# The 1e-9 added to the sums of a softmax on GpSimd instead of VectorE, in a kernel with a fixed order of instructions

## The chip, the cores and the metric

One NeuronCore of a Trainium2 chip runs the kernel. The metric is the device time of one execution in microseconds (us), as the median of several runs. The engines are TensorE (PE; its weight loads are listed apart as PEld), VectorE (DVE), ScalarE (ACT), GpSimd (POOL) and SyncE (SP), which issues all the DMAs here.

## The reference

Causal attention with a decay for 8 batches of 8 heads, 576 positions, 64 numbers a head, and behind it a mixer over tokens and over channels, all in float32:

```python
scores = scale * np.matmul(q, k.transpose(0, 1, 3, 2))
log_f = np.log(np.clip(f, 0.0001, 1.0))
cum = np.cumsum(log_f, axis=-1)
decay = cum[:, :, :, None] - cum[:, :, None, :]
scores = np.where(causal, -1000000000.0, scores + decay)
scores = scores - np.max(scores, axis=-1, keepdims=True)
attn = np.exp(scores)
attn = attn / (np.sum(attn, axis=-1, keepdims=True) + 1e-09)
out = np.matmul(attn, v)
# x: the heads side by side, 576 x 512 a batch
h = np.maximum(x.transpose(0, 2, 1) @ w_tok1, 0.0) @ w_tok2
u = x + h.transpose(0, 2, 1)
y = u + np.maximum(u @ w_ch1, 0.0) @ w_ch2
```

The 1e-9 in the last line of the softmax is what the change is about.

## The kernel before, in words

Nearly every product is made with both factors split into a high part, in TensorE's fast 32-bit format, and a low part, the rest: three matmuls where one would be (high by high, low by high, high by low). The first four heads are done in plain float32.

For each of the 64 heads, `build` describes the following steps. SP loads q and k (`raw`); their high and low parts are made (L972, L980 on GpSimd, L970 on ScalarE) and gathered by DMA into the tiles `k1`, `k2`. TensorE makes the scores of five blocks of rows, of 64 or 128 rows and 64, 192, 320, 448 and 576 columns (L1061). VectorE adds the mask and takes each row's minimum of the negated scores (`rmin`, L1068). ScalarE makes the exponentials into `pr` and their sums into `sums` (`expo`, L1075). `rec1` (L1093) adds 1e-9 to the head's five columns of sums, in a tile of 128 x 6; `rec2` (L1096) takes the reciprocals; `norm` (L1103), on GpSimd, multiplies the five blocks of exponentials by them in place. TensorE transposes the blocks (L1117); ScalarE copies out the high halves and VectorE the low ones (L729, L738); GpSimd puts the low half of the first block below its high half (L732); TensorE multiplies by the values (L1189 to L1201); ScalarE and VectorE fold the result into `xt` (L1239, L1246). Behind every four heads the token mixer of half a batch is mixed in between, and behind every eight a part of the channel mixer (L1683 to L1815). From some 562 us on only products with the channel mixer's weights are left (L1339 and on, then L1544 to L1546 and L1606 to L1608).

`rec` and `sums` exist four times (`sm = n % 4`), `pr` three times.

The order on each engine is worked out by the program while it is built. Every step is given to `Plan.op` with its engine, an assumed duration, a priority, what it reads and writes, and its buffers. `Plan.run` plays the engines' time with these assumed durations; whenever an engine is free it takes, of the steps that are ready and find their buffers, the one with the lowest priority. The instructions are then written in that order, so each engine's queue is fixed and worked off in order. The priorities come from the table `PR`: one row for each kind of step (k23, k24 and so on, numbered as the kinds appear), with one number for each of its occurrences.

Where the plan sees TensorE without work for long, the kernel writes filler matmuls, `idle` (L803), of 128 columns whose result nobody reads. Their number follows from the length of the planned gap:

```python
gap = (o.start - at_) * heads
g0, g1, g2 = GAP if o.start > 50000 else EARLY
for _ in range(PRM["FILL"] if at_ == 0 else int((gap - g0) / g1) if gap > g2 else 0):
    E["idle"](at_ == 0)
```

Of the kernel before, what the change touches and what calls it, by code (L numbers as in the profile page):

```python
# [13 lines left out]
ALU = mybir.AluOpType  # L14
# [9 lines left out]
    k0=(1,),  # L24
    k1=(1, 0,),
# [18 lines left out]
    k21=(5, 6,),
    k22=(9, 10, 21, 29,),
    k23=(1, 0, 2, 5, 4, 3, 7, 10, 6, 22, 14, 20, 29, 25, 24, 36, 37, 35, 49, 51, 53, 56, 58, 52, 73, 75, 79, 91, 89, 88, 103, 106, 105, 114, 117, 115, 135, 136, 133, 145, 149, 146, 165, 167, 171, 179, 183, 185, 199, 203, 200, 213, 215, 217, 226, 230, 228, 240, 241, 243, 260, 263, 262, 275, 280, 279, 291, 293, 297, 309, 315, 310, 322, 326, 323, 341, 346, 343, 359, 358, 363, 373, 374, 375, 387, 394, 390, 407, 409, 405, 422, 425, 424, 437, 439, 438, 451, 452, 459, 464, 467, 472, 485, 491, 486, 503, 502, 501, 518, 523, 521, 534, 535, 536, 551, 555, 553, 564, 566, 568, 587, 590, 589, 605, 607, 608, 620, 621, 619, 635, 639, 636, 652, 655, 657, 667, 677, 672, 686, 689, 688, 700, 709, 707, 725, 721, 720, 737, 735, 739, 752, 755, 756, 764, 766, 768, 780, 787, 783, 805, 806, 803, 812, 814, 820, 826, 839, 831, 846, 863, 861, 857, 859, 876, 879, 892, 889, 893, 898, 906, 911, 923, 922, 925, 929, 937, 942, 950, 951, 954, 964, 953,),
    k24=(18, 14, 17, 20, 22, 30, 26, 29, 23, 28, 38, 40, 41, 34, 37, 60, 48, 49, 55, 57, 69, 61, 64, 59, 62, 76, 77, 79, 75, 78, 92, 93, 96, 95, 97, 101, 102, 107, 94, 98, 118, 120, 121, 123, 124, 139, 134, 137, 133, 135, 153, 157, 159, 154, 156, 161, 167, 170, 165, 169, 186, 187, 189, 183, 184, 194, 201, 203, 200, 202, 219, 220, 222, 225, 226, 233, 237, 238, 239, 241, 255, 259, 260, 256, 258, 269, 270, 273, 272, 274, 284, 287, 290, 286, 288, 298, 299, 303, 300, 302, 321, 323, 325, 322, 324, 333, 340, 342, 338, 341, 353, 355, 357, 360, 361, 372, 378, 379, 374, 376, 384, 391, 392, 385, 389, 403, 408, 409, 405, 407, 424, 421, 423, 427, 428, 437, 441, 443, 440, 442, 457, 459, 461, 455, 458, 470, 472, 475, 468, 471, 491, 493, 495, 492, 494, 505, 507, 510, 506, 509, 520, 522, 523, 526, 528, 543, 535, 539, 542, 545, 556, 560, 562, 557, 559, 576, 578, 580, 571, 574, 591, 596, 597, 594, 595, 608, 609, 611, 610, 616, 628, 632, 633, 629, 631, 639, 643, 645, 646, 647, 664, 667, 670, 665, 668, 679, 680, 681, 682, 683, 692, 694, 697, 693, 696, 707, 715, 717, 712, 716, 731, 736, 738, 734, 737, 748, 756, 757, 752, 753, 767, 769, 771, 768, 770, 780, 786, 787, 784, 785, 801, 797, 799, 796, 798, 812, 809, 811, 813, 815, 827, 829, 831, 830, 832, 837, 840, 842, 843, 846, 856, 861, 862, 859, 860, 878, 879, 881, 876, 877, 884, 890, 891, 895, 896, 901, 909, 911, 906, 908, 916, 932, 934, 931, 933, 929, 928, 930, 942, 944, 947, 962, 964, 956, 959, 961, 965, 966, 975, 977, 979, 989, 992, 988, 990, 993, 995, 997, 1006, 1007, 1010, 1018, 1019, 1021, 1023, 1026, 1034, 1036, 1022, 1025,),
# [5 lines left out]
    k30=(35, 32, 34, 46, 51, 50, 66, 65, 64, 84, 81, 83,),  # L53
# [64 lines left out]
    k95=(524,),  # L118
# [1977 lines left out]
```

## Time and profile before

| | |
|---|---|
| median of 3 runs | 1024.95 us (1023.31 to 1025.09) |
| the profiled execution | 1024.19 us, its span 1022.4 us |
| TensorE busy | 1009.8 us (99%) |
| VectorE busy | 810.8 us (79%) |
| ScalarE busy | 695.1 us (68%) |
| GpSimd busy | 421.7 us (41%), none of it after some 565 us |
| DMA queue of SP | 210.99 MB, 61.6% of the 16 engines' span |
| granted TensorE clock | 1.000 |

The span runs from the first to the last instruction of the trace. The shares are averages over the whole span. The kernel has two parts with different limits, so the busy time by stage is the view to start from. An engine's idle time matters only where something later waits for it; for that there are the lists of who waited for whom, and the timeline.

### The profile page before, as it was taken

How to read it: one execution, taken by the hardware profiler on the slowest of the kernel's cores; microseconds unless marked ns; L12 is line 12 of the kernel's file. 1: busy time of each engine (PE TensorE's matmuls, PEld its weight loads, DVE VectorE, ACT ScalarE, POOL GpSimd, SP SyncE). 2: the span in 40 equal slices, each digit the busy share in tenths (PEclk: the TensorE clock that was granted, in tenths of full speed). 3: DMA queues.
4: the chain of work that ended last, by engine and by line, in shares of the span. 5: the costliest groups of instructions: out<-in, count | busy, mean ns of one | idle time of the engine just before them, and what ended most of it. 6: DMA issues, size and time to landing. Idle time of an engine off the chain costs nothing.

```text
span 1022.4 us, 19342 instructions
## 1 busy us (share of the span) xinstructions
PE 1009.8 (99%) x6230; PEld 883.1 (86%) x6230; DVE 810.8 (79%) x1932; ACT 695.1 (68%) x1708; POOL 421.7 (41%) x530
## 2 busy tenths in 40 slices
PE   9999999999999999999999999999999999999998
PEld 7588999999899999999999988888888788888886
DVE  7789889898899797887896557859669765976794
ACT  6898889888888788888886434565365446544652
POOL 6589778778787686887872100000000000000000
PEclk9999999999999999999999999999999999999999
DMA  8766798786877766553655468916832772384054
GB/s 239 252 203 215 278 305 290 280 271 235 278 250 277 278 215 225 186 206 130 237 187 211 185 189 267 298 48 211 276 104 78 224 224 82 124 250 152 21 175 145
DMA packets 110597, 212.23 MB, mean 208 GB/s; under 512 B 13296, under 2 KB 51184, under 8 KB 109472
## 3 DMA queue, kind: packets, MB, share of 16 engines
q1 hardware_dynamic: 110496, 210.99, 61.6%
q8 instruction: 50, 0.82, 0.3%
q14 instruction: 51, 0.42, 0.1%
HBM read 113.26 MB, written 44.04 MB: 154 GB/s over the span
## 4 chain that ended last, share of the span: by engine, by line
PE 84%; ACT 5%; DVE 5%; DMA 2%; issue 2%; POOL 1%; SPq 1%; POOLq 0%; DVEq 0%; ACTq 0%
PE bank L1117 8%; PE bank L1606 6%; PE bank L1544 6%; PE bank L1545 6%; PE bank L1546 6%; PE bank L1607 6%; PE bank L1608 6%; PE bank L1061 5%; PE pair L1199 3%; PE pair L1061 3%; PE pair L1201 3%; ACT pr L1075 2%; PE bank L1785 2%; PE bank L1787 2%; PE bank L1786 2%
## 5 line engine op out<-in xcount | busy, mean ns | idle before, releaser
L1103 POOL TENSOR_SCALAR pr<-pr,rec 128x192 f32<-128x192 f32 (+4 forms) x320 | 166.7, 536 | 68.0 <-DVE rec L1096 25.9
L729 ACT ACTIVATE p<-bank 128x384 fp32r<-128x384 f32 (+3 forms) x300 | 129.8, 473 | 21.5 <-PE bank L1117 19.4
L1117 PE MATMUL bank<-ident,pr 128*128 128x128 f32 (+1 forms) x960 | 139.6, 275 | 1.3 <-DVE p L738 0.4
L1075 ACT ACTIVATE pr<-bank,nmin 128x448 f32<-128x448 f32 (+3 forms) x256 | 118.0, 469 | 17.3 <-DVE nmin L1068 15.8
L1117 PEld LDWEIGHTS bank<-ident,pr 128*128 128x128 f32 (+1 forms) x960 | 106.3, 131 | 18.4 <-ACT pr L1075 2.2
L1068 DVE CUSTOM_DVE_ANT_0 bank<-bank,mask 128x448 f32<-128x448 f32 (+3 forms) x256 | 106.0, 434 | 13.6 <-PE bank L1061 8.4
L738 DVE TENSOR_TENSOR p<-bank,p 128x384 fp32r<-128x384 f32 (+1 forms) x180 | 104.6, 589 | 13.1 <-ACT p L729 12.3
L1606 PE MATMUL bank<-ring,w2r 128*128 128x512 f32 x242 | 94.4, 390 | 0.7 <-ACT ring L729 0.7
L1607 PE MATMUL bank<-ring,w2r 128*128 128x512 f32 x242 | 94.2, 389 | 0.0
L1608 PE MATMUL bank<-ring,w2r 128*128 128x512 f32 x220 | 85.6, 389 | 0.0
L1061 PE MATMUL bank<-k 128*128 128x320 f32 (+1 forms) x480 | 83.4, 302 | 1.6 <-ACT part L1820 1.1
L1201 PE MATMUL pair<-p,vv 128*128 128x512 f32 x240 | 75.5, 322 | 0.0
L980 POOL TENSOR_TENSOR hl<-raw,hl 128x1152 fp32r<-128x1152 f32 x27 | 72.6, 2689 | 1.4
L1199 PE MATMUL pair<-p,vv 128*64 128x512 f32 x240 | 69.4, 330 | 0.0
L1061 PEld LDWEIGHTS bank<-k 128*128 128x128 f32 (+1 forms) x480 | 63.0, 176 | 5.8 <-ACT part L1820 1.5
L729 ACT ACTIVATE ring<-h 128x512 fp32r<-128x512 f32 x73 | 44.3, 628 | 34.6 <-PE bank L1607 17.2
L729 ACT ACTIVATE ring<-xt 128x512 fp32r<-128x512 f32 (+1 forms) x84 | 53.0, 648 | 19.9 <-DVE xt L1754 6.2
L738 DVE TENSOR_TENSOR low<-bank,p 64x512 fp32r<-64x512 f32 (+1 forms) x120 | 52.3, 444 | 12.0 <-ACT p L729 10.1
L1075 ACT ACTIVATE pr<-pair,nmin 128x576 f32<-128x576 f32 x64 | 47.3, 739 | 17.9 <-DVE nmin L1068 15.5
L729 ACT ACTIVATE ring<-bank 128x512 fp32r<-128x512 f32 (+2 forms) x96 | 47.4, 498 | 14.5 <-PE bank L1717 6.7
L735 POOL TENSOR_TENSOR ring<-xt,ring 128x576 fp32r<-128x576 f32 x32 | 46.1, 1449 | 23.5 <-ACT ring L729 23.4
L1606 PEld LDWEIGHTS bank<-ring,w2r 128*128 128x128 f32 x242 | 45.4, 188 | 10.7 <-ACT ring L729 1.1
(200 smaller groups left out, 3050.3 us busy)
## 6 DMA issues: line engine op xcount, KB each, us to landing
k<-hl SPq DMA_DIRECT2D x180, 288.0 KB
w2r<-sd SPq DMA_DIRECT2D x80, 256.0 KB
raw<-in_qk SPq DMA_DIRECT2D x60, 288.0 KB
w2r<-wd SPq DMA_DIRECT2D x60, 256.0 KB
vr<-in_v SPq DMA_DIRECT2D x32, 320.0 KB
ud<-xt SPq DMA_DIRECT2D x8, 1152.0 KB
pd<-part SPq DMA_DIRECT2D x32, 288.0 KB
dd<-in_w_ch SPq DMA_DIRECT2D x12, 512.0 KB
```

Of the source, the lines that this page charges most:

```text
L729: nc.scalar.activation(out, in_, func, scale=scale)
L738: nc.vector.tensor_tensor(out, in_, asf(hi), op=ALU.subtract)
L1061: nc.tensor.matmul(ps[:m, of : of + w], k[:, 0, i0 : i0 + m], k[:, 1, j0 : j0 + w], start=(x == 0), stop=(fq or x == 1))
L1068: nc.vector.tensor_tensor_reduce(x, x, E["mask"][:m, a : a + w], -1.0 / D**0.5, 3e38, op0=ALU.add, op1=ALU.min, accum_out=E["nmin"][sm][:m ...
L1075: nc.scalar.activation(at(pr)[:m, poff[t] : poff[t] + w], at(buf)[:m, of : of + w], AF.Exp, bias=E["nmin"][sm][:m, t : t + 1], scale=-1.0, ...
L1103: nc.gpsimd.tensor_scalar(x, x, r, 0.0, op0=ALU.mult, op1=ALU.add)
L1117: nc.tensor.transpose(out, at(pr)[:, poff[i] + start[j] : poff[i] + end[j]], E["ident"])
L1199: nc.tensor.matmul(x[:D], at(vv)[:, v0 + j, :D], at(pb)[:, 1, c0 : c0 + w], start=False, stop=last)
L1201: nc.tensor.matmul(x, at(vv)[:, v0 + j, :], at(pb)[:, 0, c0 : c0 + w], start=False, stop=last)
L1606: nc.tensor.matmul(o_, wh[:, ms], h_, start=first and pr == 0, stop=False, skip_group_check=not first)
L1607: nc.tensor.matmul(o_, wl[:, ms], h_, start=False, stop=False, skip_group_check=not first)
L1608: nc.tensor.matmul(o_, wh[:, ms], l_, start=False, stop=pr == PH - 1, skip_group_check=not first)
```

## The change

`rec1` is given to GpSimd, with a second operation (adding 0.0) that its form there has, and an assumed duration of 190 in place of 72. The table `PR` is another one in nearly every row.

```diff
 PR = dict(
...
-    k0=(1,),
-    k1=(1, 0,),
...
+    k0=(0,),
+    k1=(0, 1,),
...
         def rec1(sm=sm):
-            nc.vector.tensor_scalar(E["rec"][sm][:, :, :2], E["sums"][sm].rearrange("p (a b) -> p a b", b=3), 1e-9, None, op0=ALU.add)
+            nc.gpsimd.tensor_scalar(E["rec"][sm][:, :, :2], E["sums"][sm].rearrange("p (a b) -> p a b", b=3), 1e-9, 0.0, op0=ALU.add, op1=ALU.add)
...
-        p.op("DVE", 72, n + o["rec"], rec1, rd=[("sums", sm, t) for t in range(NS)], wr=[("rec", sm)])
+        p.op("POOL", 190, n + o["rec"], rec1, rd=[("sums", sm, t) for t in range(NS)], wr=[("rec", sm)])
         p.op("DVE", 100, n + o["rec"], rec2, wr=[("rec", sm)])
```

`rec1` has a row of its own there (k26), with one number for each head. What the table does to the order shows on the engines' queues. In the rows below, names carry the number of the tile: `rec_92` is the third of the four `rec` tiles, `pr_184` the third `pr` tile, `bank_63` to `bank_66` the four single PSUM banks, `pair_70` and `pair_71` the double ones.

VectorE at the fifteenth head, before:

```order
L738 TENSOR_TENSOR low_191<-bank_64,p_190 64x512
L738 TENSOR_TENSOR p_189<-bank_63,p_189 128x512
L1093 TENSOR_SCALAR rec_92<-sums_88 128x3x2
L1096 RECIPROCAL rec_92<-rec_92 128x3x2
L741 SCALAR_TENSOR_TENSOR ring_162<-bank_66,ring_161 128x288
L738 TENSOR_TENSOR p_187<-bank_64,p_187 128x384
L1068 ISA pair_70,nmin_85<-pair_70,mask 128x576
L1068 ISA nmin_85 128x1
```

and now:

```order
L738 TENSOR_TENSOR p_189<-bank_66,p_189 128x512
L833 TENSOR_SCALAR dd<-dd 128x512
L1068 ISA pair_70,nmin_85<-pair_70,mask 128x576
L1068 ISA nmin_85 128x1
L738 TENSOR_TENSOR low_191<-bank_63,p_190 64x64
L1246 SCALAR_TENSOR_TENSOR xt_151<-pair_71,lower,xt_151 128x576
L1096 RECIPROCAL rec_92<-rec_92 128x3x2
L738 TENSOR_TENSOR p_185<-bank_65,p_185 128x384
```

The add (L1093) is gone from VectorE's queue, and the reciprocal (L1096) stands behind the minimum of the next head's largest block and the fold into `xt`; the instruction behind it is now the subtraction for the low half (L738). In 37 of the 64 heads L738 is the next instruction after the reciprocal.

GpSimd at the same head, before:

```order
L972 TENSOR_SCALAR hl_175<-raw_172 128x2x576
L980 TENSOR_TENSOR hl_175<-raw_172,hl_175 128x2x576
L1103 TENSOR_SCALAR pr_184<-pr_184,rec_92 128x448
L1103 TENSOR_SCALAR pr_184<-pr_184,rec_92 128x320
L732 TENSOR_SCALAR p_190<-low_191 64x576
L1103 TENSOR_SCALAR pr_184<-pr_184,rec_92 64x64
L1103 TENSOR_SCALAR pr_184<-pr_184,rec_92 128x576
L980 TENSOR_TENSOR vv_181<-vr_174,vv_181 128x10x64
L1103 TENSOR_SCALAR pr_184<-pr_184,rec_92 128x192
```

and now:

```order
L972 TENSOR_SCALAR hl_175<-raw_172 128x2x576
L980 TENSOR_TENSOR hl_175<-raw_172,hl_175 128x2x576
L1093 TENSOR_SCALAR rec_92<-sums_88 128x3x2
L732 TENSOR_SCALAR p_190<-low_191 64x576
L1103 TENSOR_SCALAR pr_184<-pr_184,rec_92 128x448
L1103 TENSOR_SCALAR pr_184<-pr_184,rec_92 128x320
L1103 TENSOR_SCALAR pr_184<-pr_184,rec_92 64x64
L1103 TENSOR_SCALAR pr_184<-pr_184,rec_92 128x576
L980 TENSOR_TENSOR vv_181<-vr_174,vv_181 128x10x64
L1103 TENSOR_SCALAR pr_184<-pr_184,rec_92 128x192
```

The add has come in between the subtraction of 1152 columns (L980) and the copy of the low half (L732), which is ahead of the head's first multiplication. Of the 64 adds, 11 stand right behind an L980 of 1152 columns, 6 behind one of the values' (640 columns) and 10 behind an L735; in 37 heads the first multiplication follows the add at once.

TensorE in front of the token mixer's transposes (L1683) of the second batch's second half, before:

```order
L1740 MATMUL bank_64<-held,ring_157 128x288
L1741 MATMUL bank_64<-held,ring_157 128x288
L1742 MATMUL bank_64<-held,ring_158 128x288
L1740 MATMUL bank_64<-held,ring_157 128x288
L1741 MATMUL bank_64<-held,ring_157 128x288
L1742 MATMUL bank_64<-held,ring_158 128x288
L1199 MATMUL pair_71<-p_187,vv_180 64x384
L1201 MATMUL pair_71<-p_187,vv_180 128x384
L1683 MATMUL bank_66<-ident,xt_151 128x128 x4
L1683 MATMUL bank_65<-ident,xt_151 128x128 x4
```

and now:

```order
L1061 MATMUL bank_66<-k_177 128x320
L1061 MATMUL bank_66<-k_179 128x320
L1061 MATMUL bank_66<-k_177 128x192
L1061 MATMUL bank_66<-k_179 128x192
L1117 MATMUL bank_63<-ident,pr_184 128x128 x3
L803 MATMUL pair_71<-lower 16x128 x21
L1683 MATMUL bank_64<-ident,xt_151 128x128 x4
L1189 MATMUL pair_71<-p_190,vv_180 128x512
L1190 MATMUL pair_71<-p_190,vv_180 128x64
```

The matmuls of the token mixer (L1740 to L1742) and of the attention that came ahead of these transposes stand elsewhere now, and 21 fillers have come in. In all there are 204 fillers instead of 168: the first 140 and the last 16 as before, and between them groups of 15, 5, 7 and 21 where there were 7 and 5.

## Rows read from the trace of the kernel before

**Rows 1.** The page's first part: busy us, share of the span, instructions.

```profile
PE 1009.8 (99%) x6230; PEld 883.1 (86%) x6230; DVE 810.8 (79%) x1932; ACT 695.1 (68%) x1708; POOL 421.7 (41%) x530
```

**Rows 2.** Busy time by stage (us, then PE, PEld, DVE, ACT, POOL; clock, DMA share).

```profile
0.00:28.00 28.00, 25.79 (x202) 19.07 (x203) 21.82 (x70) 19.96 (x56) 17.84 (x35) 1.00 0.87 242
...
60.00:562.00 502.00, 496.47 (x3796) 466.66 (x3795) 431.65 (x1249) 421.63 (x1165) 380.13 (x463) 1.00 0.68 238
...
1018.00:1022.40 4.40, 0.55 (x3) 0.13 (x1) 0.69 (x1) 0.00 (x0) 0.00 (x0) 1.00 0.32 119
```

**Rows 3.** What TensorE waited for, 28 to 562 us: total, times, longest.

```profile
PE bank L1061 <- ACT part L1820: 1.1, 1, 1.1
PE bank L1740 <- DVE p L738: 0.9, 2, 0.6
...
PE pair L803 <- ACT xt L1232: 0.3, 1, 0.3
...
PE pair L1189 <- POOL p L732: 0.2, 1, 0.2
PE pair L1189 <- DVE xt L1246: 0.2, 1, 0.2
```

**Rows 4.** The same of the weight loads, 28 to 562 us.

```profile
PEld bank L1117 <- POOL pr L1103: 0.8, 1, 0.8
```

**Rows 5.** TensorE in order of time at the fillers: start, us, [idle before].

```profile
60.59 0.58 PE L803 MATMUL pair<-lower 128*16 128x128 f32 x7 [0.25 <-ACT xt L1232]
...
364.13 0.54 PE L803 MATMUL pair<-lower 128*16 128x128 f32 x5
364.99 0.66 PE L1683 MATMUL bank<-ident,xt 128*128 128x128 f32 x4 [0.33 <-DVE p L738]
...
563.57 1.10 PE L803 MATMUL pair<-lower 128*16 128x128 f32 x16
564.51 0.37 PE L1740 MATMUL bank<-held,ring 128*128 128x288 f32 x1
```

**Rows 6.** Add and reciprocal on VectorE by form: busy us, mean ns | idle before.

```profile
L1096 DVE RECIPROCAL rec<-rec 128x6 f32<-128x6 f32 x64 | 11.9, 186 | 1.4
...
L1093 DVE TENSOR_SCALAR rec<-sums 128x6 f32<-128x6 f32 x64 | 9.8, 153 | 11.7 <-ACT pr L1075 11.1
```

**Rows 7.** GpSimd's instructions by form: busy us, mean ns | idle before.

```profile
L980 POOL TENSOR_TENSOR hl<-raw,hl 128x1152 fp32r<-128x1152 f32 x27 | 72.6, 2689 | 1.4
...
L732 POOL TENSOR_SCALAR p<-low 64x576 fp32r<-64x576 f32 x60 | 40.1, 668 | 30.6 <-DVE low L738 15.6 <-DVE rec L1096 5.8 <-ACT xt L1239 4.5
...
L972 POOL TENSOR_SCALAR hl<-raw 128x1152 fp32r<-128x1152 f32 x27 | 31.2, 1156 | 4.9 <-DMA k<-hl 3.6 <-issue 0.4 <-DMA vr<-in_v 0.3
...
L1103 POOL TENSOR_SCALAR pr<-pr,rec 64x64 f32<-64x64 f32 x64 | 21.4, 335 | 13.8 <-ACT p L729 5.6 <-PE bank L1117 4.6 <-DVE rec L1096 3.2
...
L2082 POOL MEMSET const-float32-0.0<- 128x1 f32 x1 | 0.1, 103 | 0.2 <-issue 0.2
```

**Rows 8.** Two heads' reciprocals in order of time: start, us, [idle before].

```profile
20.82 0.19 DVE L1096 RECIPROCAL rec<-rec 128x6 f32<-128x6 f32 x1
...
21.21 0.82 POOL L1103 TENSOR_SCALAR pr<-pr,rec 64x64 f32<-64x64 f32 x2 [0.15 <-DVE rec L1096]
...
118.54 2.98 POOL L980 TENSOR_TENSOR hl<-raw,hl 128x1152 fp32r<-128x1152 f32 x1
...
121.35 0.16 DVE L1093 TENSOR_SCALAR rec<-sums 128x6 f32<-128x6 f32 x1
...
121.54 0.19 DVE L1096 RECIPROCAL rec<-rec 128x6 f32<-128x6 f32 x1
```

**Rows 9.** What GpSimd and VectorE waited for, whole span: total, times, longest.

```profile
POOL pr L1103 <- DVE rec L1096: 25.9, 16, 5.4
...
DVE rec L1093 <- ACT pr L1075: 11.1, 18, 1.6
```

**Rows 10.** TensorE's only gap between 139.5 and 143 us, in order of time.

```profile
141.97 0.47 PE L1189 MATMUL pair<-p,vv 128*128 128x512 f32 x1 [0.15 <-DVE xt L1246]
```

More of the change, by code (lines that the diff above doesn't have):

```diff
@@ L149 @@
-    k126=(1365, 1369, 1371, 1373, 1374, 1363, 1366, 1368, 1370, 1372,),
+    k8=(7,),
+    k9=(0, 1,),
+    k10=(2, 5, 4, 6,),
+    k11=(1, 3, 7, 8, 9, 10,),
+    k12=(2, 4, 5, 6, 7, 13, 14, 18, 24, 29, 34, 37, 38, 39, 40, 43, 50, 51, 58, 57, 60, 63, 61, 62, 91, 111, 123, 124, 122, 121, 127, 126, 129, 125, 144, 149, 184, 183, 182, 172, 173, 181, 180, 186, 202, 211, 223, 225, 224, 220, 240, 244, 242, 239, 273, 288, 293, 290, 291, 292, 310, 313, 312, 311, 329, 339,),
+    k13=(3, 5, 10, 11, 14, 17, 23, 30, 37, 43, 53, 56, 62, 68, 84, 102, 101, 180, 183, 202, 213, 250, 252, 290, 302, 333, 349, 368, 397, 441, 472, 480, 511, 536, 563,),
@@ new lines @@
+    k14=(5, 8, 13, 16, 21, 25, 31, 42, 44, 50, 61, 64, 75, 78, 96, 118, 120, 193, 203, 218, 234, 276, 266, 326, 325, 358, 370, 390, 437, 482, 499, 530, 532, 565, 611,),
+    k15=(9, 10, 15, 19, 24, 27, 33, 45, 51, 52, 62, 66, 79, 98, 100, 135, 177, 204, 206, 230, 244, 278, 277, 345, 327, 359, 389, 481, 450, 483, 516, 546, 564, 581, 613,),
+    k17=(7, 8, 12, 15, 20, 21, 28, 40, 47, 46, 58, 60, 81, 103, 100,),
+    k18=(11, 12, 13, 14, 15, 16, 24, 34, 38, 37, 40, 45, 58, 71, 73,),
+    k19=(11, 23, 48, 59, 71, 77, 90, 103, 114, 143, 160, 179, 195, 213, 232, 258, 272, 286, 303, 328, 345, 355, 373, 392, 408, 422, 438, 455, 464, 478, 492, 503,),
@@ new lines @@
+    k43=(116, 168, 233, 296, 377, 426, 505, 543, 618, 656, 736, 776, 849, 898, 965, 978,),
+    k44=(117, 176, 246, 308, 392, 446, 527, 566, 643, 689, 767, 811, 880, 932, 996, 1009,),
+    k45=(95, 92, 91, 98, 147, 149, 151, 152, 222, 236, 215, 243, 276, 278, 277, 284, 360, 361, 366, 372, 415, 412, 416, 417, 500, 494, 504, 505, 547, 537, 539, 540, 627, 629, 622, 631, 666, 658, 659, 669, 765, 751, 747, 752, 796, 794, 798, 795, 904, 879, 890, 882, 934, 938, 933, 939, 1012, 1007, 1009, 1008, 1021, 1020, 1022, 1023,),
@@ new lines @@
+    k74=(573, 583,),
+    k75=(110, 150, 212, 289, 338,),
+    k76=(194, 226, 273, 317, 347, 396, 467, 500, 560, 597,),
+    k77=(211, 260, 307, 346, 388, 421, 500, 547, 612, 627,),
+    k78=(130, 161, 194, 210, 243, 259, 301, 330, 361, 371,),
+    k79=(128, 185, 241, 309, 362,),
+    k80=(381, 382, 383, 384, 529, 530, 531, 544, 545, 547,),
+    k81=(938, 939, 940, 970, 972, 966, 968, 987, 985, 995,),
+    k82=(975, 978, 977, 1000, 1004, 997, 999, 1024, 1022, 1028,),
+    k83=(528, 526, 527, 536, 543, 538, 537, 540, 535, 534,),
@@ new lines @@
+    k84=(525,),
+    k85=(549, 551, 553, 557,),
+    k86=(981, 983, 989, 991,),
+    k87=(1018, 1020, 1026, 1027,),
+    k88=(1030, 1033, 1035, 1055,),
+    k89=(1037, 1039, 1044, 1048, 1054, 1061, 1069, 1071, 1075, 1080,),
+    k90=(997, 999, 1002, 1004, 1016, 1020, 1027, 1028, 1034, 1042,),
+    k91=(1029, 1032, 1034, 1037, 1048, 1061, 1068, 1069, 1081, 1095,),
+    k92=(1041, 1040, 1046, 1042, 1047, 1050, 1049, 1045, 1055, 1056, 1053, 1052, 1058, 1062, 1059, 1057, 1060, 1066, 1063, 1064, 1065, 1070, 1067, 1068, 1073, 1076, 1074, 1072, 1078, 1081, 1077, 1079, 1083, 1084, 1087, 1082, 1090, 1086, 1089, 1085,),
@@ new lines @@
+    k93=(1108, 1101, 1106, 1099,),
+    k94=(593, 587, 591, 586,),
+    k95=(588,),
+    k96=(380, 379, 556, 589, 574,),
+    k97=(658, 676, 678, 682, 677, 679, 681, 716, 1053, 1054, 1056, 1058, 1111, 1113, 1115, 1117, 1077, 1079, 1083, 1085,),
+    k98=(1011, 1000, 1010, 1009, 1008, 1003, 1007, 1006, 1017, 1021, 1018, 1019, 1053, 1055, 1057, 1059, 1033, 1041, 1035, 1036,),
+    k99=(1043, 1031, 1042, 1041, 1040, 1036, 1039, 1038, 1057, 1062, 1059, 1060, 1114, 1116, 1122, 1120, 1080, 1094, 1086, 1088,),
@@ new lines @@
+    k105=(589,),
+    k106=(590,),
+    k107=(591,),
+    k108=(592,),
+    k109=(565, 563, 567, 564, 566, 575, 573, 562, 624, 621, 626, 622, 620, 623, 618, 619, 675, 671, 673, 668, 672, 674, 669, 670, 726, 724, 723, 728, 727, 725,),
+    k110=(601, 600, 597, 598, 596, 610, 599, 615, 644, 645, 662, 661, 667, 666, 658, 656, 695, 694, 717, 718, 722, 721, 710, 709, 745, 746, 767, 772, 773, 765,),
+    k111=(1126, 1129, 1139, 1142, 1227, 1211, 1239, 1225, 1334, 1310, 1345, 1330, 1439, 1416, 1451, 1437,),
@@ L150 @@
+    k126=(1363, 1366, 1371, 1373, 1374, 1362, 1364, 1368, 1370, 1372,),
     k127=(803, 802,),
```

184 lines of the change are left out of this document (69 added, 115 removed).

## The prediction

> **What bounds the kernel now.** I read the views in this order. The page's busy line first: TensorE is busy 1009.8 of 1022.4 us, VectorE 810.8, GpSimd 421.7 [rows 1]. So the time is TensorE's own stream plus its gaps, 1022.4 - 1009.8 = 12.6 us in all, and an instruction taken from VectorE is worth only what it closes of those gaps. Next the busy time by stage, which says where the gaps lie [rows 2]: 2.2 us in the first 28 us, 5.5 us from 60 to 562 (attention with the mixers in between), 3.85 us at the end, behind the last matmul, and 12.6 - 2.2 - 5.5 - 3.85 = 1.0 us in all the rest. The change touches the 64 heads, whose adds and reciprocals all lie in the first 540 us, so what it can win is the 5.5 us of the third stretch and no more. TensorE's granted clock is 1.00, the upper of its two levels, in each of these stretches, before and after the gaps, so the clock gives nothing back and takes nothing here [rows 2].
>
> Then who ended those gaps [rows 3]: seven lines of VectorE's, from 0.9 down to 0.2 us, 2.6 us together; four of ScalarE's, from 1.1 down to 0.3 us, 2.2 us together; GpSimd 0.2 us, and that by the copy of the low halves (L732), not by the multiplications (L1103). The weight loads, which run ahead of the matmuls, waited for a multiplication of GpSimd's once, 0.8 us [rows 4].
>
> Filler matmuls (L803) count as busy, so some gaps are hidden in "busy". Seven stand at 60.59 us, with 0.25 us of idle still ahead of them, and five at 364.13 us, with 0.33 us of idle still behind [rows 5]. At both places the wait was real and somewhat longer than the fillers. Sixteen at 563.57 us have no idle on either side; the next matmul starts at 564.51, so each takes 0.94 / 16 = 59 ns [rows 5].
>
> **The change part by part.**
>
> *VectorE loses 64 adds.* One is 153 ns, all are 9.8 us [rows 6]. Of the 12.7 per cent of the third stretch that VectorE is idle (502.0 - 431.65 = 70.35 us) [rows 2], TensorE felt 2.6 us. The relief can close at most those 2.6 us. The lower bound is nothing: 18 of the adds came after VectorE had waited for the exponentials, 11.1 us in all [rows 9], and there the engine was short of data and not of time. I take half, -1.3 us.
>
> *GpSimd gains 64 adds.* The trace of before has none, so I bound one. From below by GpSimd's smallest operation, a fill of 128x1, 103 ns; from above by its smallest multiplication, 64x64, 335 ns [rows 7]. Nearest in kind are the two forms with two constants: 1152 columns 1156 ns, 576 columns 668 ns, so 0.847 ns a column and 668 - 570 x 0.847 = 185 ns at 6 columns [rows 7]. That makes 64 x 185 = 11.8 us (6.6 to 21.4). In the third stretch GpSimd is idle for 502.0 - 380.13 = 121.9 us [rows 2], which is the cover: nothing on the path. Were the cover gone, all of it would be 11.8 us late, but then GpSimd would have to be the bound, and it is at 76 per cent.
>
> *The hand-over gets longer.* Before, add and reciprocal follow each other on VectorE and only the reciprocal crosses to GpSimd: it ends at 20.82 + 0.19 = 21.01 us and the multiplication starts at 21.21, a crossing of 0.2 us [rows 8]. Now the add crosses to VectorE as well, one crossing more. A head's multiplications come 0.2 us + (185 - 153) ns = 0.23 us later, if GpSimd is free. In the new order 27 of the 64 adds stand right behind one of GpSimd's long operations: 11 behind the 1152-column subtraction (mean 2.69 us) [rows 7], the others behind its shorter kin (6 at the values' low half, 10 at L735). The fifteenth head, whose rows of the order stand above, shows what that means. Its sums were ready for the add at 121.35 us while that subtraction ran from 118.54 to 121.52 [rows 8]. With the add behind it the reciprocal starts at 121.52 + 0.19 + 0.2 = 121.91 instead of 121.54, 0.37 us later. So 0.23 to 0.37 us for a head, and up to 2.7 us for a badly placed one. GpSimd already waited 25.9 us for reciprocals in 16 places [rows 9] and TensorE hardly noticed; I take nothing for it in the sum and put it into the first rival.
>
> *The order.* Every engine's order is new; matmuls, evictions and DMAs are the same in number (SP has its transfers as before, the same 64 heads are loaded and gathered), so what the queues move is the same work at other places, and I cost the moved DMAs at nothing: they are covered by loads that run a head or more ahead, and if that cover went, the wait would stand among TensorE's gaps, where now it is the lines of VectorE and ScalarE that lead [rows 3]. What differs in number is the fillers: 204 instead of 168, 36 more, in groups of 15, 5, 7 and 21 where the old order had 7 and 5 in the attention. At 59 ns that is +2.1 us of TensorE's stream. They stand directly in front of a matmul that the schedule expects to be late: either it is late, and then the wait itself is that long, or it isn't, and then the fillers cost it. Where the 21 stand, the old order has matmuls of the mixer and of the attention's products, and its trace shows one gap of 0.15 us there, at 141.97 us [rows 10]. So I take +2.1 us in full. Bounds: +2.1 us from above, as 36 x 59; from below 0, if as much is saved in short waits that get no filler.
>
> *The sum.* -1.3 + 0 + 2.1 = +0.8 us. The tail of 3.85 us and the 456 us of weight products before it hold none of what moved between engines and stay as they are. The profiled execution took 1024.19 us around its span of 1022.4; the median of the runs is 1024.95, 0.76 above it. Against the median: 1024.95 + 0.8 = 1025.8 us. A measurement of this kernel can tell about 0.2 per cent, 2.05 us, from no change (its three runs lie 1.8 us apart), so this is no change.
>
> **The rivals.**
>
> *1. Slower: the hand-over shows.* The reciprocal stands in VectorE's queue and now waits there for GpSimd. In 37 of 64 places the instruction right behind it is the subtraction that makes the low half of the transposed exponentials (L738), which TensorE's products wait for, and VectorE's outputs of that line ended most of its 2.6 us of gaps [rows 3]. Price: the fillers' 2.1 us, nothing given back by the relief, and five heads in which 0.23 to 0.37 us gets through, 5 x 0.28 = 1.4 us: +3.5 us, 1028.5. It decides from the point where the relief gives back nothing (+2.1 already passes 2.05). Were twelve of the 64 heads hit by 0.37, +6.5 us, 1031.4. For it: the 27 adds behind long operations, and the fillers, which say that the schedule itself waits longer. Against: GpSimd's 121.9 us of idle, and that the old trace has only one wait of TensorE's side for a multiplication.
> The Trainium skill speaks for this rival in two places. Its page "TensorE: Matmul & The Clock Gate" (architectural detail of the array) calls the queues of VectorE and GpSimd strictly first in, first out; the trace agrees as far as it can, since VectorE idled 11.1 us at its own adds with the subtractions queued behind them [rows 9]. "GPSIMD Engine Reference" (Key points) calls VectorE structurally about twice as fast for elementwise work. By that the add would take 2 x 153 = 306 ns rather than my 185, the five heads would lose 0.12 us more each, and this rival would come to 1029.1; the sum would stay, because GpSimd's idle time covers that too.
>
> *2. Faster: the new order closes the gaps.* If the fresh search, with a freer VectorE, closes the gaps that VectorE and ScalarE ended, 2.6 + 2.2 = 4.8 us [rows 3], and the fillers cost their 2.1, it is -2.7 us, 1022.2. It decides from 4.2 of the 5.5 us closed. For it: with 70 us of idle VectorE isn't far from its limit and each of its waits is short. Against: fillers that were added, and a stream that is 98.9 per cent full there already.
>
> *3. Nothing happens.* The add moves, but nobody waited for it, and fillers and shorter waits cancel: 1024.95. This lies inside the forecast's own range and shares its chance. That the change doesn't do what it says is ruled out by the order: 64 adds stand on GpSimd and none on VectorE.
>
> **How the numbers follow.** The forecast together with case 3 (within 2.05 us) gets 0.48: all terms are small against the threshold. Slower gets 0.34, as the one term that I can count, the fillers, is exactly as large as the threshold and only the search can give it back. Faster gets 0.18, since four fifths of the reachable gaps would have to go. The forecast's own range is 1023.0 to 1027.0. The whole range goes from 1022.0, just past rival 2 (about one chance in ten below it), to 1030.5, between rival 1 and its twelve-head bound (about one in ten above).
>
> **What would show it.** Right: TensorE's busy time up by about 2 us, to 1011 to 1012; its idle time between 60 and 562 us at 4 to 5.5; the adds on GpSimd at 0.15 to 0.25 us; VectorE's busy time down by 10 us with more idle ahead of the reciprocals; gaps at the fillers near 61, 80 and 140 us. Wrong: if the new trace shows TensorE waiting for L738 or for multiplications for more than 5 us in that stretch (rival 1), or idle time there under 2 us (rival 2), or if an add takes more than 0.4 us, or any loss beyond 562 us.

## The result and the profile after

The changed kernel takes 1036.62 us (median of 4 runs, 1035.22 to 1037.6), the kernel before 1024.13 us beside it. The ratio is 1.012, 95% interval 1.0102 to 1.0137: 12.5 us slower, beyond the upper end of the range (1030.5). The profiled execution took 1035.22 us around a span of 1033.4.

The first part of the page after, which answers to [rows 1]:

```profile
PE 1014.9 (98%) x6266; PEld 887.1 (86%) x6266; DVE 813.5 (79%) x1868; ACT 698.4 (68%) x1708; POOL 447.9 (43%) x594
```

TensorE's span of 1033.4 us is 1014.9 busy and 18.5 idle, where it was 1009.8 and 12.6. Of the 11.0 us, 5.9 are idle and 5.1 are called busy. VectorE lost 64 instructions and is busy 2.7 us longer. GpSimd gained 26.2 us for adds that were to take 11.8.

Busy time by stage in the profile after, in the columns of [rows 2], with the third stage in two pieces, and then the same two pieces of the kernel before:

```profile
0.00:28.00 28.00, 25.86 (x201) 19.17 (x201) 23.01 (x67) 20.43 (x56) 18.84 (x38) 1.00 0.86 244
...
60.00:220.00 160.00, 152.34 (x1162) 140.99 (x1162) 135.51 (x369) 132.79 (x361) 128.80 (x165) 0.99 0.71 246
220.00:562.00 342.00, 338.71 (x2596) 320.15 (x2595) 288.42 (x810) 285.33 (x790) 271.25 (x354) 1.00 0.65 227
```

```profile
60.00:220.00 160.00, 158.22 (x1212) 148.62 (x1211) 144.31 (x421) 139.84 (x388) 129.97 (x158) 1.00 0.77 264
220.00:562.00 342.00, 338.25 (x2586) 318.04 (x2585) 287.34 (x829) 281.79 (x778) 250.16 (x306) 1.00 0.64 226
```

The loss is in one piece. From 60 to 220 us TensorE's idle time goes from 1.8 to 7.7 us; from 220 to 562 it is 3.8 before and 3.3 after. Followed product by product (the start of L1189 in both traces), the changed kernel is 2 us late at 61, 5 at 117, 13 at 157, then between 8.6 and 14 us late to the last of these products (10.4 us at 551); the span is 11.0 us longer. In that piece VectorE was at 90 per cent before (144.31 of 160) and at 84 per cent in the next: this is where the other engines have least to spare.

Who ended TensorE's waits in the profile after, 28 us to the end, answering to [rows 3]:

```profile
PE pair L803 <- DVE xt L1246: 1.9, 1, 1.9
PE pair L803 <- ACT xt L1232: 1.4, 1, 1.4
PE bank L1117 <- DVE ring L738: 0.9, 5, 0.2
...
PE bank L1117 <- POOL pr L1103: 0.3, 1, 0.3
```

The two longest stand ahead of fillers, the groups of 15 and of 21. The fold (L1232 on ScalarE, L1239 and L1246 on ScalarE and VectorE) adds a head's finished product to the transposed output, which the mixer's transposes (L1683) read. By line, from 60 to 562 us: the folds (L1232 and L1246) ended 3.8 us of TensorE's idle time (0.4 before) and VectorE's L738 4.3 us (2.7 before). GpSimd's multiplications end 0.3 us. The longer of the two waits in order of time, TensorE:

```profile
166.81 2.42 PE L803 MATMUL pair<-lower 128*16 128x128 f32 x21 [1.92 <-DVE xt L1246]
```

And what VectorE did meanwhile:

```profile
164.00 0.75 DVE L1068 CUSTOM_DVE_ANT_0 pair<-pair,mask 128x576 f32<-128x576 f32 x1
...
164.68 0.52 DVE L1068 CUSTOM_DVE_ANT_0 bank<-bank,mask 128x320 f32<-128x320 f32 x1
...
165.13 0.45 DVE L1754 TENSOR_TENSOR xt<-bank,xt 128x288 f32<-128x288 f32 x1
165.50 0.35 DVE L1068 CUSTOM_DVE_ANT_0 bank<-bank,mask 128x192 f32<-128x192 f32 x1
...
165.95 0.80 DVE L1246 SCALAR_TENSOR_TENSOR xt<-pair,lower,xt 128x576 f32<-128x576 f32 x1
```

The product that this fold reads ended at 161.7 us and ScalarE's half of the fold near 163.9; the fold stands behind four row minima of the next head and one output of the mixer, and starts at 165.95, 4.2 us after its product. In the trace of before the same fold starts 1.1 us after its product. This is a matter of single places: over all 60 folds of VectorE the mean is 1.7 us in both traces. The fillers write the pair of banks that the fold reads. So they, too, wait for it: they do not fill the gap, they come after it.

The clock by stretches of the profile after (columns as above):

```profile
160.00:166.00 6.00, 4.89 (x40) 4.55 (x38) 5.69 (x19) 5.95 (x17) 4.45 (x8) 1.00 0.83 270
166.00:167.00 1.00, 0.19 (x3) 0.19 (x3) 1.00 (x4) 1.00 (x4) 0.91 (x2) 0.89 1.00 358
167.00:170.00 3.00, 3.00 (x26) 3.00 (x25) 0.91 (x3) 1.40 (x5) 3.00 (x3) 0.50 0.79 303
170.00:171.00 1.00, 1.00 (x9) 0.91 (x8) 0.25 (x1) 0.88 (x4) 0.06 (x1) 0.91 0.78 195
```

After 1.92 us without a matmul the granted clock is 0.50, the lower level of 1.2 GHz, for the 3 us from 167 to 170, and partly so in the microsecond on either side. Full busy time at half the clock is taken as half the work, so I estimate about 1.6 us, counted as busy. With 36 more fillers (2.1 us) that is 3.7 of the 5.1 us of "busy" gained; 1.4 us I can't assign.

The add itself, in the view of its line after: its shortest, median and longest time in ns, what GpSimd waited for ahead of it, and who waited for it.

```profile
L1093 POOL TENSOR_SCALAR rec<-sums x64: 252/253/1332, 21.1 to 549.9; 128x6 f32<-128x6 f32 x64
...
its engine sat idle before it (us, times) until:
  ACT pr L1075: 43.6, 34
who waited for it (us, times):
  DVE rec L1096: 15.8, 20
```

It takes 253 ns at the median and 345 at the mean (22.1 us for 64). 17 of the 64 take over 300 ns, and 14 of these stand beside L833 or L837 on VectorE, the integer operations on the mixer's weights (11 beside an L837, 3 beside an L833 alone). The Trainium skill's page "SBUF — State Buffer" (SBUF: two separate sides) says that VectorE, with two inputs from SBUF, and GpSimd take turns at a shared pair of ports, and that the loser waits for the whole instruction. L837 has two such inputs and the trace agrees there (an add of 0.80 us at 161.03 beside an L837 of 0.68); L833 has one such input, so its three are not covered by that sentence, and four adds beside L833 or L837 stayed under 300 ns.

### The profile page after: what moved, and what is told of

Same layout as the page of the kernel before. It is cut to its first block, busy times and chain, and to the rows that moved or that the text cites. A ratio compares the mean times of both kernels' runs of the same rounds, so it can differ in the third digit from the quotient of the medians.

```text
span 1033.4 us, 19378 instructions
## 1 busy us (share of the span) xinstructions
PE 1014.9 (98%) x6266; PEld 887.1 (86%) x6266; DVE 813.5 (79%) x1868; ACT 698.4 (68%) x1708; POOL 447.9 (43%) x594
## 4 chain that ended last, share of the span: by engine, by line
PE 78%; ACT 7%; DVE 5%; DMA 4%; POOL 2%; issue 2%; SPq 1%; ACTq 0%; POOLq 0%; DVEq 0%
PE bank L1117 7%; PE bank L1606 6%; PE bank L1607 6%; PE bank L1608 6%; PE bank L1544 6%; PE bank L1545 6%; PE bank L1546 6%; PE bank L1061 4%; ACT pr L1075 3%; PE pair L1061 2%; PE pair L1199 2%; PE pair L1201 2%; PE bank L1716 2%; ACT p L729 1%; PE bank L1813 1%
## 5 line engine op out<-in xcount | busy, mean ns | idle before, releaser
L1103 POOL TENSOR_SCALAR pr<-pr,rec 128x320 f32<-128x320 f32 (+4 forms) x320 | 169.7, 544 | 26.1 <-DVE rec L1096 21.7
L1075 ACT ACTIVATE pr<-bank,nmin 64x64 f32<-64x64 f32 (+3 forms) x256 | 118.1, 469 | 22.3 <-DVE nmin L1068 21.1
L738 DVE TENSOR_TENSOR p<-bank,p 128x384 fp32r<-128x384 f32 (+1 forms) x180 | 105.3, 590 | 10.8 <-ACT p L729 9.8
L1606 PE MATMUL bank<-ring,w2r 128*128 128x512 f32 x256 | 99.8, 390 | 0.4 <-issue 0.4
L1607 PE MATMUL bank<-ring,w2r 128*128 128x512 f32 x256 | 99.6, 389 | 0.0
L1608 PE MATMUL bank<-ring,w2r 128*128 128x512 f32 x228 | 88.7, 389 | 0.0
L1061 PE MATMUL bank<-k 128*128 128x320 f32 (+1 forms) x480 | 83.4, 303 | 1.4 <-DVE p L738 0.8
L980 POOL TENSOR_TENSOR hl<-raw,hl 128x1152 fp32r<-128x1152 f32 x27 | 72.7, 2692 | 1.4
L729 ACT ACTIVATE ring<-h 128x512 fp32r<-128x512 f32 x79 | 47.8, 627 | 36.3 <-DVE h L1571 12.2
L1061 PEld LDWEIGHTS bank<-k 128*128 128x128 f32 (+1 forms) x480 | 63.3, 176 | 6.0 <-DVE p L738 1.7
L738 DVE TENSOR_TENSOR low<-bank,p 64x512 fp32r<-64x512 f32 (+1 forms) x120 | 52.1, 442 | 14.9 <-ACT p L729 13.2
L1606 PEld LDWEIGHTS bank<-ring,w2r 128*128 128x128 f32 x256 | 48.1, 188 | 11.2 <-ACT w2r L729 0.8
L729 ACT ACTIVATE ring<-bank 128x512 fp32r<-128x512 f32 (+2 forms) x96 | 46.9, 497 | 15.8 <-PE bank L1717 5.6
L1607 PEld LDWEIGHTS bank<-ring,w2r 128*128 128x128 f32 x256 | 48.1, 188 | 9.9
```

Of the source, the lines that this page charges most:

```text
L729: nc.scalar.activation(out, in_, func, scale=scale)
L738: nc.vector.tensor_tensor(out, in_, asf(hi), op=ALU.subtract)
L1061: nc.tensor.matmul(ps[:m, of : of + w], k[:, 0, i0 : i0 + m], k[:, 1, j0 : j0 + w], start=(x == 0), stop=(fq or x == 1))
L1075: nc.scalar.activation(at(pr)[:m, poff[t] : poff[t] + w], at(buf)[:m, of : of + w], AF.Exp, bias=E["nmin"][sm][:m, t : t + 1], scale=-1.0, ...
L1103: nc.gpsimd.tensor_scalar(x, x, r, 0.0, op0=ALU.mult, op1=ALU.add)
L1606: nc.tensor.matmul(o_, wh[:, ms], h_, start=first and pr == 0, stop=False, skip_group_check=not first)
```

## The experiments

There are two main theories. **Order:** the new order itself leaves TensorE waiting, wherever the add is done. **Hand-over:** the way from VectorE over GpSimd and back is the loss. They come apart by doing each half of the change alone.

### The add alone, and the order alone

The first run is the kernel before, its table of order untouched, with one line changed; the second is the changed kernel with that line put back. On every engine the order of all other instructions is that of its parent.

```
-            nc.vector.tensor_scalar(E["rec"][sm][:, :, :2], E["sums"][sm]..., 1e-9, None, op0=ALU.add)
+            nc.gpsimd.tensor_scalar(E["rec"][sm][:, :, :2], E["sums"][sm]..., 1e-9, 0.0, op0=ALU.add, op1=ALU.add)
```

> The order of before, with the add of 1e-9 alone put on GpSimd (64 of them), at the same place of the program. Theory 'hand-over' (the way from VectorE over GpSimd and back holds the products of the heads, and GpSimd's add is long beside VectorE's): 1030 to 1037 us, the loss of the changed kernel or most of it. Theory 'order' (the new order of the operations itself leaves TensorE waiting between 55 and 170 us, wherever the add is done): 1022 to 1027 us. Theory 'fillers' (what is lost is their 48 products behind waits and the clock after them): as 'order', since the fillers here are those of before.

> The order of the changed kernel, with the add of 1e-9 back on VectorE. Theory 'hand-over': 1023 to 1028 us. Theory 'order': 1032 to 1037 us, with the gaps of TensorE at 62 and at 165 to 167 us still there. Theory 'fillers': 1032 to 1037 us as well, since the 15, 5, 7 and 21 fillers stay.

Measured: the add alone 1038.79 us (ratio 1.014, 1.0122 to 1.0159), somewhat above the range of either theory, the order alone 1035.97 us (1.0112, 1.0095 to 1.013). **Both halves lose, each about as much as the whole.** They don't add up, because they belong to different orders: in the order of before the hand-over costs 14 us; in the order made for it, it costs 1036.62 - 1035.97 = 0.65 us (1.2 if each is taken against the kernel before beside it), which isn't resolved, and the order costs 11.3. For the changed kernel, then, the theory of the order holds.

Their traces differ. VectorE's and TensorE's longest waits where the add alone moved:

```profile
DVE rec L1096 <- POOL rec L1093: 40.6, 39, 2.8
```

```profile
PE bank L1813 <- DVE p L738: 2.0, 2, 1.6
PE bank L1117 <- DVE low L738: 1.9, 2, 1.3
PE bank L1716 <- DVE ring L738: 1.5, 1, 1.5
PE bank L1740 <- DVE p L738: 1.3, 4, 0.6
```

VectorE stands at 39 reciprocals for 40.6 us (before, 11.1 us at 18 adds [rows 9]), and its evictions by L738 come late to TensorE, all the way from 70 to 550 us: they end 11.3 of its 16.1 us of idle time from 60 to 562 us, where it was 2.7 of 5.5 before. This is the first rival, as it was described. The changed kernel's order cut that wait to 15.8 us. TensorE's longest waits where the order alone changed are those of the changed kernel, the folds:

```profile
PE pair L803 <- DVE xt L1246: 2.1, 1, 2.1
PE pair L803 <- ACT xt L1232: 1.4, 1, 1.4
PE bank L1117 <- DVE ring L741: 1.3, 1, 1.3
```

Here the wait ahead of the 21 fillers is even a little longer than in the changed kernel, 2.1 us, and the clock does not fall behind it (columns as above):

```profile
160.00:170.00 10.00, 7.94 (x76) 7.43 (x75) 8.37 (x25) 9.66 (x29) 7.54 (x10) 1.00 0.84 274
```

The mean clock is 0.998 in all four executions of the changed kernel and 1.000 in three of the five with the order alone. A wait of this length brings the clock down in one execution and not in another, and the loss of the order does not need it.

### The fillers

From the changed kernel and from the kernel before, the fillers between 25 and 500 us of the plan are taken out:

```
-  ... int((gap - g0) / g1) if gap > g2 else 0):
+  ... int((gap - g0) / g1) if gap > g2 and not 25000 < o.start < 500000 else 0):
```

> The changed kernel without the four groups of fillers (15, 5, 7 and 21 of them) between 60 and 560 us; those at the start and the end stay. Theory 'fillers': they stand behind waits and are pure length, so 48 x 59 ns = 2.8 us less, and 1 us more where they ran at the half clock: 1032 to 1034 us. Theories 'order' and 'hand-over' say the same of the fillers, but that 8 us and more of the loss stay. If fillers did keep the clock up, the time would stay at 1035 to 1038 us and the half clock after 167 us would last longer than 4 us.

> The kernel before without its two groups of fillers (7 and 5) between 60 and 560 us. All theories: 12 x 59 ns = 0.7 us less at most, 1023 to 1025 us. If the fillers there kept the clock up, a stretch at the half clock would show near 61 or 364 us and the time would be 1 to 3 us longer.

Measured: the changed kernel without them 1039.55 us (1.0142, 1.012 to 1.0164), the kernel before without them 1025.13 us (1.001, 0.9996 to 1.0024). The theory that they are pure length falls: nothing is gained by leaving 48 out. (The 2.9 us by which the first is slower than the changed kernel are not resolved.) Where the groups of 5 and 7 had stood, near 85 us, the clock falls in the run without fillers:

```profile
84.00:88.00 4.00, 2.55 (x13) 1.73 (x12) 3.97 (x14) 2.69 (x8) 3.81 (x5) 0.89 0.45 167
88.00:92.00 4.00, 4.00 (x25) 3.56 (x22) 1.12 (x4) 2.96 (x12) 3.85 (x4) 0.69 0.12 46
```

In the changed kernel it was 1.00 in both stretches:

```profile
84.00:88.00 4.00, 3.29 (x27) 2.74 (x28) 3.97 (x14) 2.69 (x9) 3.81 (x5) 1.00 0.38 144
88.00:92.00 4.00, 3.88 (x31) 3.60 (x29) 2.65 (x8) 3.95 (x12) 3.83 (x5) 1.00 0.07 25
```

So a filler's 59 ns is not a cost to be added: it stands in for a wait. That it also keeps the clock is what this pair of traces suggests; it isn't shown in general. In the kernel before without its fillers the clock stays at 1.00 at both places where they had stood (61 and 364 us) and falls somewhere else, behind a wait of 1.41 us that ends at 28.8 us. The number of the fillers is a sign. The code places int((gap - 300) / 85) of them in a gap of over 700 ns that its own plan foresees (L473 holds the three numbers, L2058 the formula), so 15, 5, 7 and 21 stand for planned gaps of at least 1.58, 0.73, 0.90 and 2.09 us, 5.3 us in all, and the 7 and 5 of before for 1.6 us.

### What the relief and the extra work are worth by themselves

In the order of before: without the add on either engine; and with 64 adds more, on GpSimd, into a tile that nobody reads.

```
-            nc.vector.tensor_scalar(E["rec"][sm]..., E["sums"][sm]..., 1e-9, None, op0=ALU.add)
-            nc.vector.reciprocal(E["rec"][sm][:, :, :2], E["rec"][sm][:, :, :2])
+            nc.vector.reciprocal(E["rec"][sm][:, :, :2], E["sums"][sm]...)
```

```
             nc.vector.tensor_scalar(E["rec"][sm]..., E["sums"][sm]..., 1e-9, None, op0=ALU.add)
+            nc.gpsimd.tensor_scalar(E["dum"][sm]..., E["sums"][sm]..., 1e-9, 0.0, op0=ALU.add, op1=ALU.add)
```

> The kernel before without the add of 1e-9 (it is left out: the reciprocal reads the sums themselves), in the order of before. It shows what relief of VectorE alone is worth, 64 x 153 ns = 9.8 us of its time, with no hand-over. If VectorE's evictions bound the waits of TensorE, some of the 12.6 us of TensorE's idle time go: 1021 to 1024 us. If the order of before leaves VectorE slack wherever the add stands, nothing: 1024 to 1026 us.

> The kernel before, its add and reciprocal on VectorE as they were, and beside them 64 adds of the same form on GpSimd at the same place, into a tile that nobody reads. Theory 'VectorE held' (what costs 14 us when the add alone moves is VectorE, which waits at the reciprocal for GpSimd with its evictions behind it): little is lost, 1024 to 1029 us. Theory 'GpSimd's queue' (the add holds GpSimd's own evictions and multiplications until the exponentials are done): 1034 to 1040 us, most of the 14 us. TensorE's waits tell them apart too: for L738 of VectorE in the first theory, for L732 and L1103 of GpSimd in the second.

Measured: without the add 1024.25 us against 1024.67 (0.9995, 0.9984 to 1.0005). VectorE's relief is worth nothing that can be resolved in this order: the interval goes from 1.6 us gained to 0.5 us lost. With the extra adds 1029.31 us (1.0048, 1.0031 to 1.0064), 4.6 us slower and between the two forecasts, though no instruction waits for them. GpSimd has idle time in plenty, but it takes its instructions in order, and it now stops 26 times for exponentials that it didn't need; TensorE's longest wait becomes the copy by GpSimd that stands behind:

```profile
POOL dum L1094 <- ACT pr L1075: 40.7, 26, 3.8
```

```profile
PE pair L1190 <- POOL p L732: 2.7, 6, 1.0
PE bank L1717 <- DVE ring L738: 1.5, 1, 1.5
```

VectorE's L738 ends more of TensorE's idle time too, 5.6 us from 60 to 562 us where it was 2.7. So of the 14 us of the add alone about 4.6 come from GpSimd's queue. The other 9.5 or so I put down to the crossing to VectorE; that is a difference of two runs, and no run has the crossing alone.

### The reciprocal three instructions later

The kernel with the add alone moved, each reciprocal put three instructions later in VectorE's queue, so that VectorE needn't stand and wait (a function that reorders one engine's queue and keeps every dependency is added, by which the line numbers rise by 46):

```
+    def late(s):
+        for o in [o for o in s if o.fn.__name__ == "rec2"]:
+            i = s.index(o)
+            s[i : i + 4] = s[i + 1 : i + 4] + [o]
+    order = moved(order, "DVE", late)
```

> The add alone on GpSimd in the order of before, as in the run where it alone moved (1038.8 us), but with each reciprocal three instructions later in VectorE's queue. Theory 'VectorE held': the 40.6 us that VectorE waited there fall to under 15 us and the time to 1026 to 1033 us. Theory 'GpSimd's queue': the multiplications start later still, 1038 to 1044 us.

Measured: 1084.11 us (1.0577, 1.0561 to 1.0593), 45 us worse than without it: the largest miss of the study. The edit did what it should, VectorE's wait at the reciprocals falls from 40.6 to 2.3 us. But what the wait bought was an early reciprocal. From the end of a head's exponentials to the end of its reciprocal it is 0.98 us on average before, 1.37 with the add alone moved, and 3.30 here (worked out over the 64 heads of each trace, head by head). TensorE's and GpSimd's longest waits:

```profile
PE pair L1235 <- POOL p L778: 23.5, 24, 1.9
```

```profile
POOL pr L1149 <- DVE rec L1142: 59.7, 38, 5.5
```

L1149 is the multiplication (L1103 before), L778 the copy of the low halves (L732), L1235 a head's first product (L1189). GpSimd waits for the reciprocals, all of its later work slips, and TensorE waits for that. The way from the exponentials over the reciprocal to the products has little slack in this order: longer by 2.3 us than before, it goes with a loss of 59 us; shorter by 0.13 us (0.85 us where the add is left out), with no gain that can be resolved. With the add alone moved it is 0.39 us longer, but there VectorE stands as well and GpSimd's queue is held, so the 14 us aren't the price of this length alone.

### One wait of the new order taken away

The changed kernel, with the fold at 165.95 us put ahead of the row minima:

```
+    def early(s):
+        i = [i for i, o in enumerate(s) if o.fn.__name__ == "fold"][11]
+        s.insert(i - 5, s.pop(i))
+    order = moved(order, "DVE", early)
```

> The changed kernel with one instruction moved: the twelfth fold of VectorE (L1246, at 165.95 us), put five instructions ahead, before the row minima. Theory 'place of the fold': TensorE's 1.92 us idle before the 21 fillers falls under 0.5 us, the half clock after it does not come, and the time is 3 us less or more: 1032 to 1034 us. If the wait only moves to the row minima (the next head's exponentials late), 1035 to 1038 us.

Measured: 1037.55 us (1.0121, 1.0107 to 1.0136), no gain. The step did what it should: no idle time before the 21 fillers, the clock at 1.00, and the next head's product starts 2.9 us earlier than in the changed kernel. Then it is given back, in TensorE's order of time:

```profile
168.04 0.66 PE L1729 MATMUL bank<-ident,xt 128*128 128x128 f32 x4 [0.73 <-ACT pr L1121]
...
280.04 0.76 PE L1107 MATMUL bank<-k 128*128 128x320 f32 x4 [1.00 <-ACT part L1866]
```

The exponentials, whose row minima now stand behind the fold, are late: 1.8 us of the lead are left at 178. At 280 TensorE waits for ScalarE, and ScalarE for a transfer of weights:

```profile
279.02 0.66 ACT L875 ACTIVATE dd<-dd 128x512 f32<-128x512 f32 x1 [1.37 <-DMA dd<-in_w_ch]
```

The changed kernel doesn't wait there; the kernel before does, for 1.1 us (L1061 in [rows 3]). A lead that was longer than this transfer allows ended in this wait. From 287 us on 0.4 us is left, and at the end nothing. One long wait taken away is not its length gained.

### Another order for the same change

The plan that makes the order adds up costs written in the code. By that reckoning, which is no measurement, the order of before ends at 1016.0 us and that of the changed kernel at 1023.5, and TensorE stands idle 7.5 us longer, 6.3 us of it from 60 to 220 us, the piece where the trace has the loss. I searched the table of the changed kernel further (priorities altered at random and kept where the plan ends sooner), and that of the kernel before by as much. The diff is the table alone; one of its rows is shown. The third run is the first with the add's line put back on VectorE.

```
-    k26=(17, 23, 30, 39, 44, 54, 63, 66, 80, 88, ...
+    k26=(112, 45, 44, 142, 93, 74, 128, 69, 36, 85, ...
```

> The changed kernel with its table of order searched further: the plan by which the order is made reckons with its own costs 1016.0 us for the order of before, 1023.5 us for that of the changed kernel, and 1018.4 us for this one (add on GpSimd, all else as in the changed kernel). Theory 'the order found was a poor one': the time follows the plan, 5 us less than the changed kernel, 1029 to 1033 us. Theory 'the add on GpSimd costs in any order' (what the plan leaves out of it, the longer adds and the waits at the hand-over, is the loss): 1034 to 1038 us.

> The kernel before with its table of order searched further by as many steps: the plan reckons 1013.0 us where it has 1016.0 us for the order of before (add on VectorE). If the time follows the plan: 1020 to 1023 us, faster than both kernels. If the order of before fits the chip better than the plan can tell, any order found anew loses: 1026 to 1033 us.

> The order of the run searched further with the add on GpSimd, and the add back on VectorE. If the place of the add costs nothing in an order made for GpSimd, the same time as with the add on GpSimd within 2 us; if the hand-over is a cost there too, 3 us less or more.

Measured: the change in the new order 1032.92 us (1.0082, 1.0064 to 1.01); with the add back on VectorE 1031.82 us (1.0076, 1.0056 to 1.0095); the kernel before in its new order 1026.43 us (1.0014, 0.9999 to 1.0028). The changed kernel in its new order follows the plan: 5.1 us less than the changed kernel by reckoning, 3.7 us by measurement, and the intervals of the two ratios don't meet. The add's place is worth 1.1 us there, again not resolved. The kernel before in its new order does not: 3.0 us less by reckoning, and no gain. The chip's time lies 7.8 to 8.7 us above the plan's for the order of before (its times beside the other runs), and 13.1, 14.5 and 13.4 us above it for the changed kernel and for the two new orders. So the order of before is better on the chip than its plan can tell, by 5 to 7 us against each of the three, and these three orders start with that loss. What makes the difference isn't shown. No version was found that beats the kernel before.

The run with the add on GpSimd still has VectorE waiting at the reciprocals for 14.7 us, as the changed kernel for 15.8:

```profile
DVE rec L1096 <- POOL rec L1093: 14.7, 21, 2.2
```

## Why the prediction was wrong

**The failed step is "the order".** It saw "the same work at other places" and put a price on the 36 fillers alone, +2.1 us, which was its upper bound as well; the matmuls and evictions at other places had no price at all. The run with the order alone lost 11.3 us. (The moved DMAs, which it put "at nothing" by name, did cost nothing directly: from 60 to 562 us no wait of TensorE's was ended by a DMA.) What the runs show in the place of that nothing is an order in which TensorE stands longer for the other engines, for single folds above all and for L738. By the plan's reckoning 7.5 us of the changed kernel's 12.5 are foreseen waits, and the plan could have been reckoned for both tables before any run. The other 5 us the plan doesn't see, and their cause stays open; one wait taken away by itself gave nothing. The sign was in my own text, "a matmul that the schedule expects to be late", and I priced it by the filler's length instead of by the gap that calls for it (5.3 us against 1.6 before). Even that would have been too little: it adds 3.7 us, not 11.

*The relief, -1.3 us:* 0.4 us less in the run without the add, with an interval from 1.6 us less to 0.5 more. Nothing is resolved, and neither the lower bound nor the half that I took is excluded. The share of VectorE's idle time beside it was misread: 70.35 of 502 us is 14.0 per cent and not 12.7; the sum doesn't use it.

*The adds on GpSimd, 185 ns each, covered:* 345 ns at the mean, just beyond the upper bound of 335. The cover was the worse error. 121.9 us of idle time at an engine that takes its work in order is no room for an instruction that must wait for exponentials; the run with the extra adds lost 4.6 us by them.

*The hand-over, 0 in the sum:* 0.39 us a head in the old order, just above the estimate (0.23 to 0.37). What it does depends on the order. In the old one the add alone cost 14 us, some 9.5 of them by the crossing if the run with the extra adds is taken off; that is more than the twelve heads' 6.5 us of the first rival, and by that rival's mechanism. In the orders made for it, 0.65 and 1.1 us were measured, neither resolved.

*The clock, "gives nothing back and takes nothing here":* right for the trace of before, and carried over to a trace with a gap of 1.92 us, where it took about 1.6 us. In the trace with the order alone it took nothing.

*What would show it:* idle time of 4 to 5.5 us from 60 to 562 us was wrong (10.95), VectorE's busy time 10 us down was wrong (2.7 up: the adds are gone, but by line L837 takes 3.1, L738 2.3 and L833 2.3 us more), and TensorE's busy time of 1011 to 1012 was 1014.9. An add takes 253 ns at the median and 345 at the mean, where 150 to 250 was the sign of being right. Right: waits ahead of the fillers at 61 and 165 us (not at the two groups near 85), more idle time ahead of the reciprocals, and no loss beyond 562 us. The first rival had the right sign. For the changed kernel it had the wrong place: L738 and the multiplications end 4.6 us from 60 to 562 us, less than the 5 us that it asked for, and L738 ended 2.7 of them before.

## What to carry to other kernels

In a kernel whose queues are all ordered by hand or by a search, a new order has a price of its own even where every instruction stays. If a planner made it, let it reckon both orders first: here that gave 7.5 of the 12.5 us. Then look at the bounding engine's longest waits for a result that stands ready behind other work in its producer's queue, as the fold did that started 4.2 us after its product instead of 1.1 (though that one wait, taken away by itself, gave nothing here). Fillers or padding that a planner puts in mark the waits that it foresees; read the gap that calls for them, not their length. An engine's idle time covers an added instruction only where its inputs are ready when its turn comes. And do each half of such a change alone: the two halves here lost 14 and 11 us, and together 12.

## What the runs showed of the hardware

An add of 128x6 on GpSimd takes 252 to 253 ns when undisturbed, against 153 ns on VectorE, and up to 1.33 us beside other work on VectorE (1.60 us in the run with the extra adds). After 1.92 us without a matmul the granted clock was 0.50 for 3 us of full work; after 2.1 us at the same place in the run with the order alone it stayed at 1.00; and in the kernel before without its fillers it was 0.80 and 0.77 from 28 to 32 and from 32 to 36 us, behind a wait of 1.41 us. The length of one wait does not tell whether the clock falls. With the 12 fillers near 85 us the clock was 1.00, and 0.69 over 4 us in the run without fillers. A delay of TensorE is not always kept: in four of the runs (the add alone, the kernel before without fillers, without the add, and with extra adds) 1.2 to 1.4 us of it vanished at about 270 us, where the kernel before waits 1.1 us for ScalarE, which waits for a transfer of weights.
